# Two pad tiles that move the tile starts, gate weights decoded earlier in batch 0, and three subtractions one product later, in an attention and two-MLP kernel

## The chip, the core and the metric

One core of a Trainium2 chip runs the whole program. The metric is the time of the slowest core on the device in microseconds (us); with one core it is that core's time. All data is float32; f32r names the form in which TensorE takes float32 at the rate that this kernel uses.

## The reference

Eight batches of eight heads, 576 tokens, head size 64; 32 packed queries. Attention is done twice, first by the packed queries over the keys, then by the tokens over the packed result. Two MLPs over all 4608 tokens follow.

```python
def sm_attn(qq, kk, vv):
    s = scale * np.matmul(qq, kk.transpose(0, 1, 3, 2))
    s = s - np.max(s, axis=-1, keepdims=True)
    a = np.exp(s)
    a = a / (np.sum(a, axis=-1, keepdims=True) + 1e-09)
    return np.matmul(a, vv)
p_packed = sm_attn(p, k, v)
out = sm_attn(q, p_packed, p_packed)
x = np.ascontiguousarray(attn_out.transpose(0, 2, 1, 3)).reshape(B * S, H * D)
# first MLP, d_model 512, d_ff 1536
g = x @ w_gate
silu = g * (1.0 / (1.0 + np.exp(-g)))
val = x @ w_val
x = (silu * val @ w_out)
# second MLP, d_ff 2048
h = x @ w_in
g = h * np.cos(h)
out = g @ w_out
```

## The kernel before

TensorE multiplies in f32r by three passes: each operand is split into a high half (a copy on ScalarE that rounds to f32r) and a low half (a subtraction on VectorE), and high x high, high x low, low x high are added in PSUM (`PASSES`). The weights come from the host as int64 views and are decoded on the chip.

**Stage 1, attention and the first up projection (`a_up`, about 109 to 470 us for batches 1 to 7).** For each batch b the loop runs over twelve blocks f of d_ff. In each, `half` makes the gate product `pg` and the value product `pv` (L502 in batch 0, plain float32; L513 in the others, 12 f32r matmuls of 288 columns each), a silu on ScalarE (L533) and a product on VectorE (L553) give `h`, and a DMA from the POOL queue stores it. The weights of the up projection are first multiplied into the packed attention result (`a_wp`, `a_wp0_pair`, L473), so the products take the attention weights a2 as moving operand and `wp` as weights. The attention of batch b + 1 is done in the gaps: `sched` holds, for each half step k (k = 2f after pg, 2f + 1 after pv), the functions that are called there, and `attention` is handed a tuple of k for 18 steps: exponential, sum, transpose, packed product, its scaling, its transpose, second scores, turn, maximum, subtraction, exponential, sum, scaling, turn back, split, and three weight products. A split's low half is put into `pend` and issued at the next half step.

**Batch 0** (up to about 109 us) decodes the gate weights besides. There are 24 units, two for each block; `u_load` (SP queue, L315, four buffers of two units each), `u_act` (two ACTIVATEs on ScalarE, L108 and L109) and `u_dve` (two instructions on VectorE, L115 and L118) each have a counter, and `u_step(k, n)` moves one of the three on by n units. `a_wp0_pair(m)`, called in block f = 2m - 1 after the silu, multiplies the units 4m to 4m + 3 and copies the product to `wpp`, which the next two blocks use. PSUM has four tiles of two banks for all of this.

**Stage 2, the first down projection (470 to 740 us).** Strassen's scheme with seven products over five sets of tokens (`SETS`, four of 512 columns and one of 256), in the order `ORDER` = 0, 4, 6, 1, 2, 3, 5. `strassen` issues 36 f32r matmuls (L633); `sums1` issues on VectorE the subtractions of input blocks (L613) that product `i` of the set has in its table; `prep` makes the halves of the next product's input (L86 on ScalarE, L87 on VectorE), and `evict` follows. The input blocks `hr` are loaded from DRAM on the SP queue. The weights of product 0 lie in pool `da`, those of 3 and 5 in `db`, those of 4, 6, 1 and 2 in `gates` (`W1_AT`). The g tiles, the moving operand, lie in `da` and `db`.

**Stage 3, the second MLP (740 to 1497 us).** 48 steps p: seven products of six f32r matmuls with 384 columns (L959; weights `up` in pool `late`, moving operand `xs` in pool `xs`), a cosine on ScalarE and VectorE, and the down projection in pieces of twelve matmuls with 512 columns (L974; both operands in `late`). Inside a step, products and downs alternate.

**Where tiles start.** Pools are laid from the left (`cst`, `st`, then `att`, later `da`, `db`, `late`) and from the right (`gates`, `ups`, later `xs`). `cst` and `st` hold many small tiles before the left pools. Counted within a partition, all large tiles of the left pools start at 384 bytes past a multiple of 512, all large tiles of the right pools at 480 past one; a tile's inner pieces lie a multiple of 512 bytes from its start, but for a2 (multiples of 128).

Of the kernel before, what the change touches and what calls it, by code (L numbers as in the profile page):

```python
# [45 lines left out]
def attention_mlp_kernel(ctx: ExitStack, tc: tile.TileContext, qT, kT, vP, pP, wgv, w12, out):  # L46
# [7 lines left out]
    def pool(n, side=None):  # L54
        kw = {"side": side} if side else {}
        return stage[n].enter_context(tc.tile_pool(name=n, bufs=1, reuse_waits="tile", **kw))

    att = pool("att")
    gw, ups = pool("gates", "right"), pool("ups", "right")
# [277 lines left out]
    def u_step(k, n):  # L337
        for _ in range(n):
            (u_load, u_act, u_dve)[k](u_next[k])
            u_next[k] += 1  # L340
# [147 lines left out]
    def a_up(b, sched):  # L488
# [31 lines left out]
        for f in range(NF1):  # L520
# [32 lines left out]
            DVE.tensor_tensor(out=h_, in0=s_, in1=pv[:, :, :HS], op=ALU.mult)  # L553
            nc.gpsimd.dma_start(out=h1[f, :, S * b:S * b + S], in_=h_.rearrange("p c n -> p (c n)"))
            if b == 0:
                u_step(0, 1)
                u_step(1, 1)
                if f == 0:
                    u_step(2, 1)
                del wp[0, f]  # L560
            side(2 * f + 1)
# [40 lines left out]

    def sums1(s_, i):
        todo = {
            0: [((0, 1), (0, 1), (0, 0), fp) for fp in range(3)],
            2: [((1, 1), (1, 1), (0, 1), fp) for fp in range(3)],
            3: [((0, 0), (1, 1), (0, 0), fp) for fp in range(3)],
            4: [((1, 0), (1, 0), (1, 1), 0)],
            5: [((1, 0), (1, 0), (1, 1), fp) for fp in (1, 2)],
        }  # L610
        for to, x, y, fp in todo.get(i, ()):
            to, x, y = (raw1[s_, k, t, fp] for k, t in (to, x, y))
            DVE.tensor_tensor(out=to, in0=x, in1=y, op=ALU.subtract)  # L613
# [111 lines left out]
    with tc.manual_schedule():  # L725
# [46 lines left out]
            s2_mul(u)  # L772
            s2_back(0, u)
        s2_split(0)
        u_step(1, 2)
        u_step(2, 3)

        def loads(b, what):
# [11 lines left out]
        def first_scores(sched, b, at_k):  # L790
            put(sched, at_k[0], lambda: s1_mm(b))
            put(sched, at_k[1], lambda: s1_max(0), lambda: s1_max(1))
# [12 lines left out]
        for b in range(B):  # L805
            sched = {}
            if b == 0:
                for k, what in ((0, "k"), (6, "v"), (10, "q")):
                    put(sched, k, loads(1, what))
                first_scores(sched, 1, (4, 5))  # L810
                attention(sched, 1, (6, 8, 8, 10, 11, 12, 14, 15, 16, 17, 17, 18, 19, 20, 20, 16, 18, 21))
                first_scores(sched, 2, (22, 23))
                for k, what in ((17, "k"), (22, "v")):
                    put(sched, k, loads(2, what))
# [1 line left out]
            else:  # L816
# [4 lines left out]
                if b == 1:  # L821
                    put(sched, 2, loads(2, "q"))
                if b < B - 1:
                    attention(sched, b + 1, (0, 3, 3, 5, 6, 8, 10, 11, 12, 13, 14, 16, 17, 18, 19, 15, 17, 20))
                    for k, what in ((4, "k"), (8, "v"), (13, "q")):
                        put(sched, k, loads(b + 2, what))
                    if b < B - 2:
# [283 lines left out]
```

## Time and profile before

| | us |
|---|---|
| median of 3 runs | 1499.68 (1497.85 to 1500.71) |
| the profiled execution | 1502.94 |
| its span | 1501.1 |
| TensorE (PE) busy | 1468.8 |
| VectorE (DVE) busy | 1084.3 |
| ScalarE (ACT) busy | 850.0 |

The prediction's sum is made against the profiled execution. In the rows, PE is the matmuls, PEld the weight loads that overlap them, L12 a line of the kernel before. A matmul's own duration holds its run through the array, which overlaps the next one's; the time that it costs is the distance from its start to the next start. "PEclk" is the granted share of TensorE's full clock of 2.4 GHz; 0.50 is its lower level, 1.2 GHz. Idle time in square brackets stands with what ended it.

### The profile page before, as it was taken

To read this page: it belongs to the slowest core of one execution; us is meant where nothing else is said; L and a number is where in the kernel's file an instruction comes from. 1 tells how busy PE (TensorE), PEld (TensorE's weight loads), DVE (VectorE), ACT (ScalarE), POOL (GpSimd) and SP (SyncE) were. 2 spreads that over 40 slices of the span, in tenths; PEclk is the share of its full clock that TensorE was granted. 3 is DMA by queue.
4 is the path that set the end of the run, shared out by engine and by line. 5 is a ranking of instruction groups with operands and counts; after the bars stand their busy time and mean duration, and the time that the engine had idled before them with its cause. 6 is when DMAs were issued, how large, how long until landed. Compare 5 with 4: busy or idle time off the path is not lost.

```text
span 1501.1 us, 25026 instructions
## 1 busy us (share of the span) xinstructions
PE 1468.8 (98%) x9352; PEld 1262.1 (84%) x9352; DVE 1084.3 (72%) x1767; ACT 850.0 (57%) x1496; POOL 123.7 (8%) x230
## 2 busy tenths in 40 slices
PE   8999999999998999999999999999999999999998
PEld 6558878887887888898889989999999999999997
DVE  6567788788774788988776866776676686677654
ACT  5757666666653456554575646646465564664642
POOL 0002222222221011011000000000000000000000
PEclk9999999999999999999999999999999999999999
DMA  8938778877697558355495585576657558556641
GB/s 318 312 112 322 249 263 302 293 254 266 235 359 281 182 188 288 124 199 194 133 365 169 197 291 179 174 239 204 213 189 249 170 187 287 186 175 197 203 154 42
DMA packets 140937, 335.62 MB, mean 224 GB/s; under 512 B 15249, under 2 KB 25489, under 8 KB 140817
## 3 DMA queue, kind: packets, MB, share of 16 engines
q1 hardware_dynamic: 120720, 262.19, 52.7%
q0 software_dynamic: 20096, 71.84, 12.5%
q8 instruction: 74, 1.21, 0.3%
q14 instruction: 47, 0.38, 0.1%
HBM read 252.71 MB, written 81.26 MB: 222 GB/s over the span
## 4 chain that ended last, share of the span: by engine, by line
PE 81%; DVE 5%; ACT 4%; issue 2%; DMA 2%; SPq 0%; POOL 0%; DVEq 0%; ACTq 0%; POOLq 0%
PE acc L974 26%; PE p L959 23%; PE o L633 16%; PE pv L513 6%; PE pg L513 6%; PE wp L473 2%; DMA hr<-h 1%; DMA h<-h 1%; DVE wp L99 1%; DVE h L553 1%; PE pp L210 1%; ACT silu L533 0%; DVE d L287 0%; PE pv L502 0%; ACT wp L96 0%
## 5 line engine op out<-in xcount | busy, mean ns | idle before, releaser
L974 PE MATMUL acc<-wd,g 128*128 128x512 f32 x1728 | 418.1, 392 | 0.0
L959 PE MATMUL p<-xs,up 128*128 128x384 f32 x2016 | 379.1, 339 | 3.1 <-issue 1.6
L974 PEld LDWEIGHTS acc<-wd,g 128*128 128x128 f32 x1728 | 323.2, 188 | 61.3
L959 PEld LDWEIGHTS p<-xs,up 128*128 128x128 f32 x2016 | 359.1, 188 | 14.8 <-issue 1.9
L633 PE MATMUL o<-g,w 128*128 128x512 f32 (+1 forms) x1260 | 265.6, 373 | 4.3 <-DVE g L87 4.2
L633 PEld LDWEIGHTS o<-g,w 128*128 128x128 f32 x1260 | 220.6, 189 | 49.0 <-DVE g L87 5.5
L937 ACT ACTIVATE t<-c,quarter 128x384 f32<-128x384 f32 x144 | 88.5, 614 | 201.5 <-DVE c L1047 195.7
L513 PEld LDWEIGHTS pg<-a,wp 128*128 128x128 f32 x1008 | 137.4, 188 | 27.5 <-issue 10.9
L86 ACT ACTIVATE g<-hr 128x1024 fp32r<-128x1024 f32 (+1 forms) x105 | 101.9, 975 | 97.8 <-PE o L633 58.8
L513 PE MATMUL pg<-a,wp 128*128 128x288 f32 x1008 | 152.3, 300 | 3.2 <-DVE h L553 2.9
L513 PEld LDWEIGHTS pv<-a,wp 128*128 128x128 f32 x1008 | 137.7, 188 | 16.7 <-DVE w2c L398 3.0
L513 PE MATMUL pv<-a,wp 128*128 128x288 f32 x1008 | 150.6, 298 | 0.2
L87 DVE TENSOR_TENSOR g<-hr,g 128x1024 fp32r<-128x1024 f32 (+1 forms) x105 | 114.2, 1115 | 40.4 <-ACT g L86 40.2
L553 DVE TENSOR_TENSOR h<-silu,pv 128x576 f32<-128x576 f32 x96 | 71.5, 745 | 68.9 <-PE pv L513 21.9
L533 ACT ACTIVATE silu<-pg 128x576 f32<-128x576 f32 x96 | 62.5, 651 | 97.2 <-PE pg L513 84.7
L1042 DVE TENSOR_TENSOR u<-v,p 128x384 f32<-128x384 f32 x48 | 26.6, 554 | 120.8 <-PE p L959 120.1
L947 DVE TENSOR_TENSOR g<-t,g 128x384 fp32r<-128x384 f32 x192 | 106.1, 553 | 8.6 <-ACT g L934 8.5
L939 DVE TENSOR_TENSOR t<-t,k 128x384 f32<-128x384 f32 x192 | 106.2, 553 | 3.4 <-ACT k L943 1.8
L940 ACT ACTIVATE t<-t 128x384 f32<-128x384 f32 x192 | 98.2, 512 | 2.5 <-DVE t L939 2.4
L934 ACT ACTIVATE g<-t 128x384 fp32r<-128x384 f32 x192 | 98.6, 513 | 0.4 <-DVE t L945 0.4
L988 DVE TENSOR_TENSOR oacc<-oacc,acc 128x512 f32<-128x512 f32 x108 | 73.8, 684 | 34.6 <-PE acc L974 34.6
L943 ACT ACTIVATE k<-t 128x384 int32<-128x384 f32 x192 | 97.9, 510 | 0.0
(106 smaller groups left out, 1476.1 us busy)
## 6 DMA issues: line engine op xcount, KB each, us to landing
up<-w2u SPq DMA_DIRECT2D x336, 256.0 KB, 3.1
wd<-w2d SPq DMA_DIRECT2D x96, 512.0 KB, 6.1
h<-h POOLq DMA_DIRECT2D x96, 288.0 KB, 4.4
hr<-h SPq DMA_DIRECT2D x48, 512.0 KB, 6.9
raw<-in_w SPq DMA_DIRECT2D x44, 512.0 KB, 4.3
raw<-in_wgv SPq DMA_DIRECT2D x24, 512.0 KB, 6.4
w2u<-w2p POOLq DMA_DIRECT2D x24, 512.0 KB, 5.1
w<-w1u SPq DMA_DIRECT2D x21, 512.0 KB, 10.2
```

The costliest lines, as they stand in the source:

```text
L86: ACT.activation(out=hi, in_=src, func=AF.Copy)
L87: eng.tensor_tensor(out=lo, in0=src, in1=hi.bitcast(F32), op=ALU.subtract)
L513: PE.matmul(out=p_[:, c, :HS], lhsT=w[:, u, x, o:o + 128], rhs=a2[b][:, u, y, HS * c:HS * c + HS], start=(n == 0), stop=(n == 5),)
L633: PE.matmul(out=acc[:, m, :N], lhsT=wd1[n, fp][:, j, 256 * x + 128 * m:256 * x + 128 * m + 128], rhs=g1[n, fp][:, y, j, :], start=(first a ...
L934: ACT.activation(out=three["g"][:, 0, :], in_=three["t"], func=AF.Copy)
L937: ACT.activation(out=now["t"], in_=now["h"], func=AF.Identity, scale=1.0 / TWO_PI, bias=quarter)
L939: DVE.tensor_tensor(out=one_["t"], in0=one_["t"], in1=one_["k"], op=ALU.subtract)
L940: ACT.activation(out=one_["t"], in_=one_["t"], func=AF.Sin, scale=SIN_SCALE)
L943: ACT.activation(out=now["k"], in_=now["t"], func=AF.Copy)
L947: DVE.tensor_tensor(out=three["g"][:, 1, :], in0=three["t"], in1=three["g"][:, 0, :].bitcast(F32), op=ALU.subtract)
L959: PE.matmul(out=out, lhsT=w[:, u, 128 * k:128 * k + 128], rhs=x[:, v, k, :], start=(first and k == 0 and i == 0), stop=(last and k == 1 an ...
L974: PE.matmul(out=acc, lhsT=gs[p, a, t][:, x, o:o + 128], rhs=wd[j, f][:, y, :], start=(f == 0 and n == 0), stop=(f == 3 and n == 2),)
```

## The change

Two tiles that nothing reads are allocated: 120 floats at the right end, ahead of `gates`, and 32 floats in `cst`. With them all large tiles of both sides start at a multiple of 512 bytes, and a2's inner pieces at multiples of 128. Batch 0's `u_step` calls move units on earlier: one unit more on ScalarE ahead of the loop, and in the second half of f = 1, 2 and 3 one unit more for the load and for ScalarE and one for VectorE; the total of 24 is the same. Batch 1's loads and attention steps stand up to two half steps earlier. In batches 2 to 7 the split and the third weight product stand one half step earlier. The three subtractions that `sums1` made with product 0 of a set are made with product 1 in that order (number 4).

```diff
+    pad = ctx.enter_context(tc.tile_pool(name="pad", bufs=1, side="right"))
+    pad.tile([128, 120], F32, name="right_pad")
+    cst.tile([128, 32], F32, name="left_pad")
...
             if b == 0:
-                u_step(0, 1)
-                u_step(1, 1)
-                if f == 0:
+                u_step(0, 2 if f in (1, 2, 3) else 1)
+                u_step(1, 2 if f in (1, 2, 3) else 1)
+                if f in (0, 1, 2, 3):
                     u_step(2, 1)
...
         todo = {
-            0: [((0, 1), (0, 1), (0, 0), fp) for fp in range(3)],
+            1: [((0, 1), (0, 1), (0, 0), fp) for fp in range(3)],
...
         s2_split(0)
-        u_step(1, 2)
+        u_step(1, 3)
         u_step(2, 3)
...
-                first_scores(sched, 1, (4, 5))
+                first_scores(sched, 1, (3, 4))
...
-                    attention(sched, b + 1, (0, 3, 3, 5, 6, 8, 10, 11, 12, 13, 14, 16, 17, 18, 19, 15, 17, 20))
+                    attention(sched, b + 1, (0, 3, 3, 5, 6, 8, 10, 11, 12, 13, 14, 16, 17, 18, 18, 15, 17, 19))
```

What stands in a row on ScalarE in batch 0, from the silu of f = 2 on; `dec` and `wg` are a gate unit's two steps, E the exponentials of batch 1's first scores, wpp the copy of a pair's product. Before:

```order
L533 ACTIVATE silu_482<-pg_475 128x576
L108 ACTIVATE dec_486<-raw_454 128x512
L109 ACTIVATE wg_456<-raw_454,low3_87 128x2x256
L108 ACTIVATE dec_518<-raw_454 128x512
L109 ACTIVATE wg_471<-raw_454,low3_87 128x2x256
L533 ACTIVATE silu_536<-pg_529 128x576
L465 ACTIVATE wpp_443<-wp_538 128x1024
L108 ACTIVATE dec_551<-raw_484 128x512
L109 ACTIVATE wg_550<-raw_484,low3_87 128x2x256
L184 ACT_TABLE_LOAD
L184 ACTIVATE E_562,sm_564<-s1_489,nm_523 128x576
```

Here the silu of f = 3 (the second one) comes after two units. The same place of the changed kernel, whose lines stand four further down:

```order
L537 ACTIVATE silu_515<-pg_508 128x576
L112 ACTIVATE dec_519<-raw_480 128x512
L113 ACTIVATE wg_518<-raw_480,low3_92 128x2x256
L112 ACTIVATE dec_552<-raw_480 128x512
L113 ACTIVATE wg_551<-raw_480,low3_92 128x2x256
L112 ACTIVATE dec_555<-raw_548 128x512
L113 ACTIVATE wg_518<-raw_548,low3_92 128x2x256
L188 ACT_TABLE_LOAD
L188 ACTIVATE E_560,sm_562<-s1_490,nm_532 128x576
L188 ACTIVATE E_564,sm_566<-s1_491,nm_536 128x576
L537 ACT_TABLE_LOAD
L537 ACTIVATE silu_575<-pg_568 128x576
```

Three units, both exponentials and two table loads now stand ahead of the silu of f = 3; the exponentials stood after it.

On VectorE at the last gate units of batch 0, around f = 7 and 8; mx2 is the maximum of the second scores and d1 <- d1,mx2 its subtraction. Before:

```order
L266 TENSOR_REDUCE mx2_834<-d1_786 128x36
L115 SCALAR_TENSOR_TENSOR wg_782<-dec_831,wg_782 128x2x256
L118 SCALAR_TENSOR_TENSOR wg_782<-raw_780,wg_782 128x2x256
L553 TENSOR_TENSOR h_854<-silu_829,pv_847 128x576
L99 TENSOR_TENSOR wp_845<-wp_836,wp_845 128x2x512
L271 TENSOR_TENSOR d1_786<-d1_786,mx2_834 128x1152
L115 SCALAR_TENSOR_TENSOR wg_816<-dec_857,wg_816 128x2x256
L118 SCALAR_TENSOR_TENSOR wg_816<-raw_780,wg_816 128x2x256
```

After:

```order
L119 SCALAR_TENSOR_TENSOR wg_734<-dec_773,wg_734 128x2x256
L122 SCALAR_TENSOR_TENSOR wg_734<-raw_752,wg_734 128x2x256
L257 STREAM_TRANSPOSE d1_789<-s2_790 128x576
L257 STREAM_TRANSPOSE d1_789<-s2_791 128x576
L119 SCALAR_TENSOR_TENSOR wg_754<-dec_786,wg_754 128x2x256
L122 SCALAR_TENSOR_TENSOR wg_754<-raw_752,wg_754 128x2x256
L557 TENSOR_TENSOR h_836<-silu_815,pv_829 128x576
L270 TENSOR_REDUCE mx2_839<-d1_789 128x36
L275 TENSOR_TENSOR d1_789<-d1_789,mx2_839 128x1152
```

The last two units stood after the maximum and after the subtraction; now both stand ahead of the maximum.

On VectorE where stage 2 begins; h is the last product of stage 1, g the low halves that `prep` makes, hr the subtractions of `sums1`, p the additions of `evict`. Before:

```order
L553 TENSOR_TENSOR h<-silu,pv 128x576
L87 TENSOR_TENSOR g<-hr,g 128x1024
L613 TENSOR_TENSOR hr<-hr 128x1024 x3
L87 TENSOR_TENSOR g<-hr,g 128x1024 x6
L646 TENSOR_TENSOR p<-p,o_5766 128x512 x2
```

After:

```order
L557 TENSOR_TENSOR h<-silu,pv 128x576
L91 TENSOR_TENSOR g<-hr,g 128x1024 x4
L617 TENSOR_TENSOR hr<-hr 128x1024 x3
L91 TENSOR_TENSOR g<-hr,g 128x1024 x3
L650 TENSOR_TENSOR p<-p,o_5768 128x512 x2
```

The three subtractions stood ahead of the second product's three halves and now stand behind them.

## Rows read from the trace of the kernel before

**Rows 1.** Page, part 1: busy time, share of the span, instructions.

```profile
PE 1468.8 (98%) x9352; PEld 1262.1 (84%) x9352; DVE 1084.3 (72%) x1767; ACT 850.0 (57%) x1496; POOL 123.7 (8%) x230
```

**Rows 2.** Stretches: length, busy time by engine (count), PEclk, DMA share, GB/s. Stage 3.

```profile
740.30:1496.70 756.40, 753.34 (x3745) 680.35 (x3743) 515.69 (x982) 418.33 (x887) 1.08 (x2) 1.00 0.63 205
```

**Rows 3.** Page, part 5: groups by line, busy us, mean ns | idle before.

```profile
L974 PE MATMUL acc<-wd,g 128*128 128x512 f32 x1728 | 418.1, 392 | 0.0
L959 PE MATMUL p<-xs,up 128*128 128x384 f32 x2016 | 379.1, 339 | 3.1 <-issue 1.6
...
L633 PE MATMUL o<-g,w 128*128 128x512 f32 (+1 forms) x1260 | 265.6, 373 | 4.3 <-DVE g L87 4.2
...
L513 PE MATMUL pv<-a,wp 128*128 128x288 f32 x1008 | 150.6, 298 | 0.2
```

**Rows 4.** Stretches of L633 alone, PE: products 3,5,0; 6,1,2; 0; 6,1,2 (256 columns).

```profile
518.42:542.91 24.49, 24.49 (x110) 1.00 0.71 257
551.34:575.83 24.49, 24.49 (x106) 1.00 0.45 159
651.42:655.73 4.31, 4.31 (x37) 1.00 0.44 172
660.15:672.97 12.82, 12.82 (x110) 1.00 0.46 154
```

**Rows 5.** Timeline of PE in stage 3: start, length, instructions.

```profile
1215.48 3.35 PE L959 MATMUL p<-xs,up 128*128 128x384 f32 x18
1218.67 2.91 PE L974 MATMUL acc<-wd,g 128*128 128x512 f32 x12
1221.41 2.28 PE L959 MATMUL p<-xs,up 128*128 128x384 f32 x12
1223.53 2.92 PE L974 MATMUL acc<-wd,g 128*128 128x512 f32 x12
1226.29 2.28 PE L959 MATMUL p<-xs,up 128*128 128x384 f32 x12
```

**Rows 6.** Timeline of PE in stage 1.

```profile
363.20 1.76 PE L513 MATMUL pv<-a,wp 128*128 128x288 f32 x12
364.80 1.75 PE L513 MATMUL pg<-a,wp 128*128 128x288 f32 x12
```

**Rows 7.** Waits of PE from 20 to 109 us: total, times, longest.

```profile
PE wp L473 <- DVE wg L118: 7.1, 7, 2.9
```

**Rows 8.** Timeline of PE in batch 0; in brackets the idle time before.

```profile
35.54 1.06 PE L473 MATMUL wp<-wg,ppT 64*32 64x512 f32 x8 [0.99 <-DVE wg L118]
36.78 1.06 PE L473 MATMUL wp<-wg,ppT 64*32 64x512 f32 x8 [0.18 <-DVE wg L118]
...
92.11 3.63 PE L473 MATMUL wp<-wg,ppT 64*32 64x512 f32 x24 [2.92 <-DVE wg L118]
```

**Rows 9.** Stretches in batch 0; the last three numbers are PEclk, DMA share, GB/s.

```profile
64.00:68.00 4.00, 4.00 (x91) 2.56 (x84) 0.37 (x1) 2.63 (x4) 0.00 (x0) 0.60 0.83 251
...
92.00:96.00 4.00, 3.89 (x25) 0.93 (x26) 1.88 (x4) 3.03 (x4) 0.00 (x0) 0.50 0.02 4
96.00:100.00 4.00, 4.00 (x13) 2.98 (x13) 0.93 (x2) 0.90 (x1) 0.00 (x0) 0.76 0.00 0
```

**Rows 10.** Groups by line, shapes apart: a gate unit's steps on ScalarE, a table load.

```profile
L109 ACT ACTIVATE wg<-raw,low 128x512 int32<-128x512 uint8 x24 | 18.3, 761 | 0.0
...
L108 ACT ACTIVATE dec<-raw 128x512 f32<-128x512 f32 x24 | 16.0, 669 | 2.2 <-DMA raw<-in_wgv 2.2
...
L184 ACT ACT_TABLE_LOAD x7 | 9.0, 1283 | 0.4 <-DVE nm L176 0.3
```

**Rows 11.** Timeline at the head of stage 2, VectorE and PE.

```profile
482.02 4.62 DVE L87 TENSOR_TENSOR g<-hr,g 128x1024 fp32r<-128x1024 f32 x4
...
483.30 28.97 PE L633 MATMUL o<-g,w 128*128 128x512 f32 x116 [4.16 <-DVE g L87]
```

**Rows 12.** Stretch of set 0's second product; L633 alone, PE and PEld.

```profile
478.74:493.12 14.38, 10.22 (x37) 7.84 (x36) 0.88 1.06 394
```

More of the change, by code (lines that the diff above doesn't have):

```diff
@@ L807, in attention_mlp_kernel @@
             if b == 0:
-                for k, what in ((0, "k"), (6, "v"), (10, "q")):
+                for k, what in ((0, "k"), (4, "v"), (8, "q")):
                     put(sched, k, loads(1, what))
-                first_scores(sched, 1, (4, 5))
-                attention(sched, 1, (6, 8, 8, 10, 11, 12, 14, 15, 16, 17, 17, 18, 19, 20, 20, 16, 18, 21))
+                first_scores(sched, 1, (3, 4))
+                attention(sched, 1, (5, 7, 7, 9, 10, 11, 13, 14, 15, 16, 16, 18, 19, 20, 21, 16, 18, 20))
                 first_scores(sched, 2, (22, 23))
```

## Prediction

> **What bounds the kernel now.** I read the busy times first: TensorE holds 98% of the span [rows 1], and in the last stage it holds 753.34 of 756.40 us [rows 2]. So only two things can shorten the program: a shorter matmul, or a stretch in which TensorE waits or runs at a lower clock. Then I read the groups by line for the counts: 1728 and 2016 matmuls in the last stage, 1260 in stage 2, 2 x 1008 in stage 1 [rows 3]. All these are f32r; 7020 of them.
>
> Next I looked at how long one such matmul takes from start to start, for each place of its operands in the memory. The tile starts are in the section on the kernel: left pools start at 384 past a multiple of 512 bytes, right pools at 480. Stage 2 is the test, since one line there draws its weights from both. In 24.49 us, 110 matmuls were seen with weights at 384 (products 3, 5, 0) and 106 with weights at 480 (6, 1, 2); the moving operand starts at 384 in both. Two were in flight at the edge, so 108 and 104: 226.8 against 235.5 ns [rows 4]. The same with 256 columns: 4.31 us for 36 is 119.7 ns, 12.82 us for 108 is 118.7 ns [rows 4]. The order of work and the shapes are equal; the place is what differs. The 384-384 pairs lie on a line: (226.8 - 119.7) / 256 = 0.418 ns a column, and 226.8 - 512 x 0.418 = 12.8 ns fixed, say 13.
>
> In stage 3 the moving operand xs starts at 480 and the weights at 384: 18 + 12 matmuls of 384 columns take 3.19 + 2.12 us, 177.0 ns each; the downs take 2.74 and 2.76 us for 12, 229.2 each, though their operands both start at 384 [rows 5]. By the line they would take 160.5 + 13 = 173.5 and 226.8. In stage 1 both operands start at 480 or 128 bytes steps from it, and 12 matmuls take 1.60 us, 133.3 ns [rows 6]; the line gives 120.4 + 13 = 133.4. So an f32r matmul costs its columns plus 13 ns where weights and moving data sit alike against 128 bytes, and something else where they don't.
>
> Then the waits. In batch 0 TensorE waits 7.1 us in seven pieces for decoded gate weights [rows 7]; the first two, 0.99 and 0.18, and the last and longest, 2.92, are shown [rows 8]. Around them the granted clock falls from 2.4 towards 1.2 GHz: 0.60 in 64 to 68 us, 0.50 in 92 to 96, 0.76 in 96 to 100 [rows 9]. At the head of stage 2 it waits 4.16 us for the low half of the second product's input, which VectorE could write only at 482.02, after sums whose data had landed late [rows 11]; that product takes 14.38 us at a mean clock of 0.88 [rows 12].
>
> **Part 1, the pads.** Two tiles that nothing reads; no instruction. Afterwards all large tiles start at 0 against 512 bytes, so weights and moving data sit alike everywhere. No row shows f32r at 0, so this is bounded from the rows. The value I take is that 0 behaves as 384 does with 384, since that is the nearest row in kind (weights and moving data alike, the same line and shape):
> - L959: (173.5 - 177.0) x 2016 = -7.1 us.
> - L974: (226.8 - 229.2) x 1728 = -4.1 us. These start alike already; I put their excess down to the stream of products that they alternate with, a guess.
> - L633, products 4, 6, 1, 2 (576 matmuls of 512 columns): (226.8 - 235.5) x 576 = -5.0 us; 144 of 256 columns: +0.1.
> - L513: 133.3 to 133.4, nothing.
>
> Sum -16 us. From below: the fixed 13 ns goes as well (a rival). From above: 0 is a bad place (a rival), or no place matters (a rival). For VectorE, ScalarE and DMA I take nothing: no wait that ends late hangs on their speed by so little. The trace bears on a rule here. The Trainium skill, "SBUF — State Buffer", section "Who interferes with whom", gives TensorE two read ports of its own, one for weights and one for moving data, and says that "PE and ACT never wait on anyone"; its 16-byte lines divide 384 and 480 alike. By that the pads would change nothing. The 8.7 ns of [rows 4] speak against it.
>
> **Part 2, decoding ahead in batch 0.** One unit more before the loop, and one more on each queue in the second half of f = 1, 2, 3; in all still 24 units. By the order, the unit that pair 5 needs stood behind the softmax subtraction on VectorE and now stands before the maximum; for pairs 2 to 5 all units are queued a half step or more before TensorE asks. Pair 1's waits stay (VectorE's queue up to there is the same): 7.1 - 0.99 - 0.18 = -5.9 us. The low clock follows these gaps: 0.40 x 4 + 0.50 x 4 + 0.24 x 4 = -4.6 us [rows 9].
>
> What is late next: on ScalarE three units of 0.669 + 0.761 us, two exponentials and two table loads of 1.283 us [rows 10] now stand between the silu of f = 2 and that of f = 3. The three units and the loads alone are 6.9 us, where TensorE has some 7 us of work (two half products of f = 2 and one of f = 3 at 2 us, the pair at 1). Two of the four PSUM tiles hold the first scores until the exponentials are done, so the second half of f = 3 and then the input of f = 4 (a copy behind that silu) wait; the copies of the transposed weights wait behind f = 3's three units. I put these new waits at 2 us, bounds 0 and 6. The loads go earlier too: SP issues the gate units 9 to 23 and the v and q tiles of batch 1 up to two steps sooner, and behind a load that waits for its buffer stand those tiles. DMA engines were busy 0.83 in 64 to 68 us and 0.02 in 92 to 96 [rows 9], so they end early enough to be pulled forward by some 10 us. Batch 0: -5.9 - 4.6 + 2 = -8.5 us, bounds -12 and -4.
>
> **Part 3, sums a product later.** The four low halves now stand before the three sums. The first needs nothing that comes late (its copy on ScalarE stands ahead of the waits), so TensorE should go on at 478.74, where the first product ends. A product with weights alike is 36 x 226.8 ns = 8.2 us, so 14.38 - 8.2 = -6.2 us [rows 4, 12], the low clock within it. The sums' next reader is the second set of sums, after product 6's input: the data came by 482, three sums and three halves at 1.2 us each (4.62 us for four, [rows 11]) end near 487, when product 4 ends. In sets 1 to 4 the sums move from one product to the next, which then holds some 11 us of VectorE work against 8.2; three tiles of input stand ready, so I take 0, bound +1 a set.
>
> **Part 4, batches 2 to 7.** Split and third weight product half a step earlier in six batches. Each moved product brings its copy on ScalarE and its low half of 1.2 us on VectorE ahead of an h product, whose bank a matmul then waits for. Either way under 0.7 us a batch: I take 0, bounds -3 and +4.
>
> **Sum.** -16 - 8.5 - 6.2 = -31 us. The profiled execution took 1502.94 us (span 1501.1); 1472. The median of the runs stands 3.26 us lower: 1469.
>
> **Rivals.**
> - *The place doesn't matter at 0.* What I read as place is a pattern of pools. For it: one line, two pools. Against: the same split shows in every set. Parts 2 and 3 alone: 1499.7 - 14.7 = 1485. Chance 0.17.
> - *The 13 ns goes too.* A start 128 bytes off the 512 would then cost it. Against: it is the same at 384 with 256 and 512 columns, as a fixed cost of a new weight would be. The excess over columns is now 16.5 x 2016 + 15.2 x 1728 + 21.5 x 576 + 13 x (432 + 252 + 2016) = 107 us; all gone, 1499.7 - 107 - 15 = 1378. Chance 0.08. The Trainium skill, "TensorE: Matmul & The Clock Gate", section "Back-to-back issue gap", has a warm gap of N / 2.4 + 2.5 ns; by that 7020 x 2.5 = 18 us of it would stay, an estimate: 1396. No row here shows f32r so near its columns.
> - *Slower: alike at 0 is a collision.* Weights and moving data then start in the same 512 bytes, and each f32r matmul pays what the 480 weights pay now, 21.5 ns over its columns: L959 +5.0 x 2016 = 10, L974 +6.3 x 1728 = 11, L633 +8.7 x 432 = 4, L513 +8.6 x 2016 = 17; 42 - 15 = +27, 1527. It decides from 15 us / 7020 = 2.1 ns a matmul. Against: alike at 384 is the good case. Chance 0.08.
> - *The decoding moves a wait instead of ending it.* ScalarE's block before the silu of f = 3 holds TensorE for 6 us or more, the clock falls again, and batch 0 gains about nothing: 1477. Chance 0.12.
>
> **How the numbers follow.** The forecast, 1469, has 0.55; its own range, by the bounds of the parts, is 1456 to 1482. The first and the last rival lie close above it, so 1455 to 1489 leaves out the two rivals of part 1 at either end and a little more, 0.2. A measurement of this kernel tells 0.2%, 3 us, from no change. Faster by that: 0.55 + 0.17 + 0.08 + 0.12 less a little, 0.90; within: 0.02; slower: 0.08.
>
> **What would show it.** Right: in stage 2 both windows hold the same number of matmuls, 24.5 us for 108; products of 18 in 3.12 us and downs of 12 in 2.72; no wait for a gate weight after 37 us and a clock of 1.00 from 60 to 100 us, stage 1 beginning some 8 to 10 us sooner; the second product of stage 2 in 8.2 us. Wrong: counts that stay at 110 and 106 (no effect of place), 1.60 us for 12 in stage 1 falling well under that (the 13 ns moves), or a gap before f = 4 of batch 0 longer than the one before pair 5 was.

## The result, and the profile after

The changed kernel takes 1478.63 us in the median (1477.73 to 1480.73), the kernel before 1499.37 beside it: a ratio of 0.9864, 95% interval 0.9847 to 0.9881. That is 20.7 us less, where 31 had been forecast. The interval is some 2.5 us wide to either side, and those of the runs below are much the same; what is said of smaller differences rests on the traces. The profiled execution took 1480.73 us, its span is 1478.6.

The stages, by the first matmul of each in the two traces, the tail from the start of the last one (us):

| | before | after | difference | forecast |
|---|---|---|---|---|
| batch 0 | 108.90 | 96.16 | -12.7 | -8.5 |
| stage 1 | 361.64 | 361.54 | -0.1 | 0 |
| stage 2 | 269.73 | 261.53 | -8.2 | -11 |
| stage 3 | 756.39 | 754.91 | -1.5 | -11 |
| tail | 4.49 | 4.46 | 0 | 0 |

The differences add up to -22.5 and not to -20.7, since the profiled execution of the kernel before lay further above the median of its runs (3.3 us) than that of the changed kernel (2.1). And the -8.2 of stage 2 hold a loss that belongs to the entry of stage 3: by the starts, the last product of stage 2 takes 10.94 us until the first product of stage 3, where it took 8.16. Without these 2.78 us stage 2 gained 11.0, as forecast.

Busy time and the three costliest groups of f32r matmuls, from the page after (parts 1 and 5; its lines stand four further down than before's in [rows 1, 3]):

```profile
PE 1456.0 (98%) x9352; PEld 1257.3 (85%) x9352; DVE 1082.6 (73%) x1767; ACT 849.8 (57%) x1496; POOL 123.7 (8%) x230
...
L978 PE MATMUL acc<-wd,g 128*128 128x512 f32 x1728 | 419.1, 392 | 0.0
L963 PE MATMUL p<-xs,up 128*128 128x384 f32 x2016 | 378.3, 338 | 3.9 <-issue 2.6
...
L637 PE MATMUL o<-g,w 128*128 128x512 f32 (+1 forms) x1260 | 258.9, 368 | 0.0
```

The 4.3 us wait of the first down projection [rows 3, 11] is gone. The group of the downs (the pieces of the second MLP's down projection) became 1.0 us longer, not shorter, and the products of stage 3 have a wait of 2.6 us.

Stage 2, the two stretches that answer to the first two of [rows 4]: matmuls of L637 alone (length, busy and count, PEclk, DMA share, GB/s), products 3, 5, 0 and then 6, 1, 2.

```profile
498.51:522.99 24.48, 24.48 (x110) 1.00 0.71 257
531.15:555.63 24.48, 24.48 (x110) 1.00 0.43 157
```

Equal counts, as the prediction wanted. From start to start, a matmul of 512 columns in stage 2 now takes 226.7 ns in all seven products. Products 4, 6, 1 and 2 had taken 8.43 us for 36, or 234.2 ns, not the 235.5 that the prediction read from the counts in its window. And set 0's second product, which took 14.38 us [rows 12], takes 8.16 at full clock:

```profile
465.87:474.03 8.16, 8.16 (x38) 6.76 (x37) 1.00 1.05 407
```

Stage 3, PE's timeline at the place in a step that answers to [rows 5]: 12 products, 12 downs.

```profile
1199.64 2.27 PE L963 MATMUL p<-xs,up 128*128 128x384 f32 x12
1201.75 2.92 PE L978 MATMUL acc<-wd,g 128*128 128x512 f32 x12
1204.51 2.27 PE L963 MATMUL p<-xs,up 128*128 128x384 f32 x12
1206.62 2.92 PE L978 MATMUL acc<-wd,g 128*128 128x512 f32 x12
```

12 products take 2.11 us, 175.8 ns each (177 before), and 12 downs 2.76, 230 each (229.2 before); 173.5 and 226.8 had been forecast. Cut by place in the step, the starts of the trace show why. A product that follows a product takes 173.3 ns a matmul, each of its six. A product that follows a down takes 171, 175, 177, 185, 176, 182: 177.6 in the mean. The twelve of a down that follows a product take 229, 233, 236, 224, 231, 236, 228, 233, 231 and then 227, 227, 227. The pattern repeats to a nanosecond through the stage. So the line of 13 ns plus columns holds in a settled stream, and after each change of width six products or nine downs are off it.

Batch 0, two stretches of the trace before and two of after (the columns are length, busy time of PE, PEld, DVE, ACT and POOL with counts, PEclk, DMA share, GB/s). Before:

```profile
0.00:60.00 60.00, 52.59 (x456) 37.00 (x457) 36.19 (x71) 37.05 (x59) 3.40 (x14) 1.00 0.91 323
60.00:108.90 48.90, 43.90 (x350) 25.70 (x349) 31.49 (x42) 27.38 (x38) 3.79 (x7) 0.90 0.49 167
```

After:

```profile
0.00:60.00 60.00, 52.91 (x533) 37.31 (x534) 41.43 (x79) 42.40 (x68) 3.41 (x14) 1.00 0.93 342
60.00:96.16 36.16, 36.16 (x274) 22.46 (x272) 26.20 (x34) 21.98 (x29) 3.79 (x7) 1.00 0.49 195
```

From 60 us on TensorE no longer waits, and its clock no longer falls. The waits of PE in batch 0 from 20 us on (total, times, longest) show what came in place of the 7.1 us of [rows 7]:

```profile
PE pv L506 <- ACT E L188: 1.6, 1, 1.6
...
PE wp L477 <- DVE wg L122: 0.8, 2, 0.7
```

One wait for the exponentials of the first scores, which hold PSUM while ScalarE decodes, is new; it is the wait that the prediction took at 2 us.

How much low clock the waits bring differs from one execution to the next. Five traces hold batch 0 as it was (the kernel before and four of the runs below), each with the same 7.1 us of waits: batch 0 takes 108.9, 105.7, 106.3, 109.1 and 105.4 us in them, with 10.2, 3.4, 3.4, 10.2 and 0 us at 1.2 GHz. Six traces hold the new order: 96.2, 96.3, 97.4, 97.7, 96.1 and 98.3 us. Their means lie 10.1 us apart, so some 2.6 of the 12.7 are owed to the two traces that the table compares.

What the prediction had not looked at is the entry of stage 3. PE's timeline, after:

```profile
707.83 8.78 PE L637 MATMUL o<-g,w 128*128 128x512 f32 x38
719.23 11.06 PE L963 MATMUL p<-xs,up 128*128 128x384 f32 x46 [2.62 <-issue]
```

and before:

```profile
740.27 1.21 PE L959 MATMUL p<-xs,up 128*128 128x384 f32 x6
743.05 3.24 PE L959 MATMUL p<-xs,up 128*128 128x384 f32 x17 [1.57 <-issue]
```

Before, the first product started at once and the second waited 1.57 us; now the first waits 2.62. The waits end 0.1 us behind the last additions of stage 2, which read the last accumulator. VectorE's timeline has them, after and then before:

```profile
717.85 1.27 DVE L650 TENSOR_TENSOR p<-p,o 128x512 f32<-128x512 f32 x2
...
741.68 1.28 DVE L646 TENSOR_TENSOR p<-p,o 128x512 f32<-128x512 f32 x2
```

By the order in which the kernel's PSUM tiles come free, that accumulator lies in the first pair of banks in the changed kernel, and the first product of stage 3 is given the first bank; before, it lay in the last pair, which the second product was given. The trace doesn't show banks; a run below tests this. In the profiled execution the granted clock was at 1.2 GHz behind this gap, from 718.6 to 725.4 us:

```profile
718.60:725.40 6.80, 6.17 (x19) 6.20 (x20) 1.12 (x3) 0.49 (x1) 1.08 (x2) 0.50 0.94 309
```

A matmul of 384 columns takes 320 ns from start to start in this stretch instead of 175, and the start of the stretch falls into the wait; added up, the low clock cost 2.9 us. The mean clocks of the other three executions, 1.000, 1.000 and 0.999, leave room for none or part of that.

### The profile page after: what moved, and what is told of

Read it like the earlier page. It is cut to its first block, busy times and chain, and to the rows that moved or that the text cites. A ratio compares the mean times of both kernels' runs of the same rounds, so it can differ in the third digit from the quotient of the medians.

```text
span 1478.6 us, 25027 instructions
## 1 busy us (share of the span) xinstructions
PE 1456.0 (98%) x9352; PEld 1257.3 (85%) x9352; DVE 1082.6 (73%) x1767; ACT 849.8 (57%) x1496; POOL 123.7 (8%) x230
## 4 chain that ended last, share of the span: by engine, by line
PE 85%; DVE 6%; ACT 5%; issue 3%; DMA 1%; POOL 0%; SPq 0%; ACTq 0%; DVEq 0%; POOLq 0%
PE acc L978 27%; PE p L963 23%; PE o L637 17%; PE pv L517 6%; PE pg L517 5%; PE wp L477 2%; PE pv L506 1%; PE pg L506 1%; DVE wp L103 1%; PE pp L214 1%; DVE d L291 1%; DMA h<-h 1%; ACT wp L100 1%; PE s L247 1%; DVE af L298 1%
## 5 line engine op out<-in xcount | busy, mean ns | idle before, releaser
L637 PE MATMUL o<-g,w 128*128 128x512 f32 (+1 forms) x1260 | 258.9, 368 | 0.0
L637 PEld LDWEIGHTS o<-g,w 128*128 128x128 f32 x1260 | 219.4, 189 | 39.2
L951 DVE TENSOR_TENSOR g<-t,g 128x384 fp32r<-128x384 f32 x192 | 105.7, 551 | 8.6 <-ACT g L938 8.4
L944 ACT ACTIVATE t<-t 128x384 f32<-128x384 f32 x192 | 98.3, 512 | 2.5 <-DVE t L943 2.4
```

The costliest lines, as they stand in the source:

```text
L637: PE.matmul(out=acc[:, m, :N], lhsT=wd1[n, fp][:, j, 256 * x + 128 * m:256 * x + 128 * m + 128], rhs=g1[n, fp][:, y, j, :], start=(first a ...
L944: ACT.activation(out=one_["t"], in_=one_["t"], func=AF.Sin, scale=SIN_SCALE)
L951: DVE.tensor_tensor(out=three["g"][:, 1, :], in0=three["t"], in1=three["g"][:, 0, :].bitcast(F32), op=ALU.subtract)
```

## The experiments

### The parts alone

**The pads alone** (`pads_only`): the kernel before with

```diff
+    pad = ctx.enter_context(tc.tile_pool(name="pad", bufs=1, side="right"))
+    pad.tile([128, 120], F32, name="right_pad")
+    cst.tile([128, 32], F32, name="left_pad")
```

> The kernel before with the two pad tiles alone; nothing else is changed. By the prediction's first part, -16 us against the kernel before: 7.1 on the seven products of stage 3, 4.1 on its downs, 5.0 in stage 2. By the theory formed from the two traces (a start in the same place brings a matmul down to its columns plus 13 ns only in a settled stream, and the first nine or so matmuls after a change between 384 and 512 columns stay off that line wherever their operands start): about -6 us, with stage 2 at 226.7 ns a matmul of 512 columns in all seven products, the first product after a down still near 177.6 ns a matmul, the one behind it at 173.3, and the downs near 230. If the gain seen came from the schedule alone and the place does nothing, 0.

Measured: 1494.07 us against 1500.20, ratio 0.9962 (0.9947 to 0.9977): -6.1. By start-to-start means of the trace L633 gives (226.8 - 231.1) x 1008 + (120.1 - 119.4) x 252 = -4.2, the products of stage 3 (175.2 - 176.7) x 2016 = -3.0, the downs (230.1 - 229.5) x 1728 = +1.1. The sum is -6.1; that it meets the measured time to 0.1 is luck, since that is known to some 2 us. The theory of the settled stream holds; the -16 do not.

**Batch 0 alone** (`batch0_only`): the kernel before with the `u_step` calls and the tables for batch 1 as in the change.

```diff
-                u_step(0, 1)
+                u_step(0, 2 if f in (1, 2, 3) else 1)
...
-                attention(sched, 1, (6, 8, 8, 10, 11, 12, 14, 15, 16, 17, 17, 18, 19, 20, 20, 16, 18, 21))
+                attention(sched, 1, (5, 7, 7, 9, 10, 11, 13, 14, 15, 16, 16, 18, 19, 20, 21, 16, 18, 20))
...
```

> The kernel before with batch 0's calls that move gate units on and batch 1's attention steps as in the changed kernel; no pads, no change to the sums. By the prediction's second part -8.5 us, bounds -12 to -4. By the trace of the changed kernel batch 0 ends 12.7 us sooner, and the entry of stage 3 is about 1 us later than before (its first product writes the PSUM bank that the last accumulator of stage 2 holds, which this schedule alone brings about), with up to 3.4 us more where the clock falls behind that gap: -12 to -8 us. By the rival that decoding only moves the wait: 0.

Measured: 1492.40 against 1500.20, ratio 0.9956 (0.9942 to 0.9970): -7.8. Batch 0 ends at 96.34 us in its trace, as in the changed kernel, so decoding ahead needs no pads. And the entry of stage 3 is the bad one here too:

```profile
725.68 1.98 PE L633 MATMUL o<-g,w 128*128 128x512 f32 x8
730.28 6.00 PE L959 MATMUL p<-xs,up 128*128 128x384 f32 x24 [2.62 <-issue]
```

With the pads alone and with the sums alone the first product starts at once, so it is this part of the change that brings the wait. How it does so is argued from the kernel: the other order of steps in batch 1 makes PSUM tiles come free in another order, the four tiles rotate differently from there on, and the rotation is still off 600 us later.

**The sums alone** (`sums_only`):

```diff
-            0: [((0, 1), (0, 1), (0, 0), fp) for fp in range(3)],
+            1: [((0, 1), (0, 1), (0, 0), fp) for fp in range(3)],
```

> The kernel before with the first subtractions of each set one product later; no pads, batch 0 as before. By the prediction's third part -6.2 us: the second product of stage 2 takes 8.2 us instead of 14.38 where the weights lay alike; here they still start at 480, so 36 x 235.5 ns = 8.5 us, -5.9, with no low clock at its place. If the wait goes on to the second set of sums or to product 6, it comes back there and the gain is 0 to -3.

Measured: 1493.29 against 1500.78, ratio 0.9946 (0.9932 to 0.9960): -7.5. The first three products run through:

```profile
468.00 25.20 PE L633 MATMUL o<-g,w 128*128 128x512 f32 x108
```

The second takes 8.43 us (476.18 to 484.61), 5.95 less than the 14.38; stage 2 takes 262.75 us instead of 269.73. Nothing is late next: in sets 2 to 4 the second product, too, is 0.2 to 0.4 us shorter, which makes most of the last 1.0 us.

The three runs add up to -21.4 us, and the whole change gave -20.7. The edit of batches 2 to 7 was not run alone. That it is worth little rests on stage 1's length: 361.64 us before, 362.05 with batch 0's part alone, 361.54 with the whole change.

### What "alike" means

**Both sides at 384** (`pads_384`): the right pad has 24 floats, no left pad.

```diff
+    pad.tile([128, 24], F32, name="right_pad")
```

> The kernel before with one pad of 24 floats at the right end: the tiles of the right pools move from 480 to 384 past a multiple of 512 bytes, the left ones stay at 384; nothing else is changed. If it counts that weights and moving operand start alike, the same gain as with both sides at 0, -5 to -8 us, and stage 2 at 226.7 ns in all seven products. If the multiple of 512 itself counts, the products whose both operands moved only from 480 to 384 gain nothing beyond what the kernel before has where both start at 384; that is the same 226.7 in stage 2, but 12 matmuls of stage 1 and the 384 columns of stage 3 would stay above what both sides at 0 give.

Measured: 1494.44 against 1500.20, ratio 0.9963 (0.9950 to 0.9976), the same as with both at 0. Stage 2 (226.8), products (175.3) and downs (230.1) agree with the pads' run to 0.1 ns. The multiple of 512 is nothing special.

**The right side at 0, the left at 384** (`pads_mixed`): the right pad of 120 floats alone.

```diff
+    pad.tile([128, 120], F32, name="right_pad")
```

> The kernel before with the right pad of 120 floats alone: right pools at 0, left pools at 384 past a multiple of 512 bytes, so weights and moving operand start alike against 128 bytes and differ against 512; nothing else is changed. If 128 bytes count: -5 to -8 us as with both at 0. If 512 bytes count: within 2 us of the kernel before, with products 4, 6, 1 and 2 of stage 2 still near 235 ns a matmul.

Measured: 1494.20 against 1500.20, ratio 0.9960 (0.9945 to 0.9975). The total, -6.0, is what "128 bytes count" had expected, and its reason is another. In stage 2 the same work takes unequal time (L635 is this kernel's L633; first products 6, 1, 2, then 3, 5, 0):

```profile
489.17:514.36 25.19, 25.19 (x110) 1.00 0.39 132
514.36:538.84 24.48, 24.48 (x109) 1.00 0.70 257
```

108 matmuls take 25.19 us with the starts 128 bytes apart, 233.2 ns each, against 226.7. So 128 bytes are not enough. But stage 3 is shorter than in any kernel so far, 751.31 us:

```profile
734.99:1486.30 751.31, 748.18 (x3745) 677.69 (x3743) 515.16 (x982) 418.30 (x887) 1.08 (x2) 1.00 0.63 207
```

Its downs, whose own operands had not moved, went from 229.5 to 227.9 ns a matmul; what had moved are the products ahead of them. The second of the two small kernels below tests whether that is the cause.

**Streams by place** (`probe_place`): a small kernel of its own.

```python
def stream(name, w, m, N, count):
    for i in range(count):
        if i % 12 == 0:
            acc = ps.tile([128, 512], F32, tag="b", name=name)
        wo = w // 4 + 128 * (i % 6)
        mo = m // 4 + 512 * (i % 12)
        PE.matmul(out=acc[:, :N], lhsT=W[:, wo:wo + 128], rhs=X[:, mo:mo + N],
                  start=i % 12 == 0, stop=i % 12 == 11)
```

> No part of the reference is computed; it writes zeros and runs streams of 48 f32r matmuls of one width back to back, each with its own starts of weights and moving operand against a multiple of 512 bytes (s512_w384m0 is 512 columns, weights at 384, moving operand at 0), with 12 matmuls at 0 and 0 between them. If only the difference of the two starts counts, and against 512 bytes: columns times 0.418 plus 13 ns (226.7, 173.3 and 133.3 ns for 512, 384 and 288) wherever both start alike, at 384 or 480 or 64 as at 0, and 2 to 9 ns more at most of the other pairs; a difference of 128 with 384 columns near 175.5, as the run with the right pad alone shows it. If the difference against 128 bytes counts: (384, 0), (128, 0), (256, 0) and (0, 384) at 226.7 too. If the multiple of 512 itself counts: only (0, 0) on the line. If the 13 ns belong to the place: some pair falls below 220 for 512 columns.

PE's timeline of its first streams of 512 columns (the names lose their last number: these are weights, moving operand at 0, 0; 384, 384; 480, 384):

```profile
23.15 11.04 PE L47 MATMUL s_w0m<-X,W 128*128 128x512 f32 x48
34.03 2.89 PE L47 MATMUL base<-X,W 128*128 128x512 f32 x12
36.76 11.05 PE L47 MATMUL s_w384m<-X,W 128*128 128x512 f32 x48
47.65 2.89 PE L47 MATMUL base<-X,W 128*128 128x512 f32 x12
50.38 11.39 PE L47 MATMUL s_w480m<-X,W 128*128 128x512 f32 x48
...
61.60 2.91 PE L47 MATMUL base<-X,W 128*128 128x512 f32 x12
```

From a stream's start to the start behind it: 10.88, 10.89 and 11.22 us for 48, or 226.7, 226.9 and 233.8 ns. All pairs, worked out in this way (a few matmuls behind each change of place are in the means):

| moving start minus weight start, modulo 256 bytes (pairs weights/moving) | 512 columns, ns | 384 columns, ns |
|---|---|---|
| 0 (0/0, 384/384, 256/0, 480/480, 64/64) | 226.7 to 227.5 | 173.3 to 173.9 |
| 32 (0/32) | 233.4 | 173.3 |
| 64 (0/64) | 229.2 | 173.2 |
| 96 (0/96, 384/480) | 233.6, 233.4 | 176.6, 176.5 |
| 128 (0/384, 384/0, 128/0) | 232.4 to 233.2 | 175.9, 176.0 |
| 160 (96/0, 480/384) | 234.2, 233.9 | 173.5, 173.4 |
| 192 (64/0, 96/32) | 233.3, 233.4 | 176.6, 174.7 |
| 224 (32/0) | 233.2 | 173.4 |
| 240 (16/0) | 226.7 | 173.5 |

The first three expectations each fail in part. It is the difference of the starts, but modulo 256: 256/0 lies on the line, the one pair that tells 256 from 512 there. One pair, 96/32, doesn't fit into that at 384 columns. No pair falls under 226.7, so at 512 columns the 13 ns do not belong to the place. With 288 columns every pair lies between 131.5 and 133.4 ns. The line would give 133.3; the pairs with a difference of 0 take 131.6 to 131.7, so the line doesn't hold for this width.

**Two widths in turn** (`probe_switch`): the same small kernel, with groups of two widths.

> No part of the reference is computed; it writes zeros and runs groups of f32r matmuls of two widths in turn, with starts as the name tells (p384x18m128_512x12: 18 of 384 columns with the moving operand at 128, 12 of 512 at 0), without any other engine at work. If the change of width itself sets the excess of stage 3: one width alone stays on the line (173.3, 226.7); 18 of 384 and 12 of 512 in turn give about 230 ns over the twelve and 174.7 over the eighteen, as in stage 3; groups of 42 and 36 show the same excess in nanoseconds at each change, and one of each in turn is worst. If the rest of the kernel (transfers, VectorE, ScalarE) causes it: both widths on the line in every case. If the starts of the products set what the downs behind them pay, as the run with the right pad alone suggests (227.9 for downs whose own operands had not moved): the case with the moving operand at 128 gives near 228 where both at 0 gives 230.

PE's timeline; a case holds 108 matmuls of 384 columns and 72 of 512, and d has both operands of both widths at 0, n has the starts of the kernel before, p and s the moving operand of the 384 columns at 128 and at 64:

```profile
97.43 35.60 PE L65 MATMUL d384x_512x<-X,W 128*128 128x384 f32 x180
132.87 5.60 PE L65 MATMUL base<-X,W 128*128 128x512 f32 x24
...
319.02 33.36 PE L65 MATMUL l512s_512s<-X,W 128*128 128x512 f32 x144
352.22 5.65 PE L65 MATMUL base<-X,W 128*128 128x512 f32 x24
...
398.61 35.72 PE L65 MATMUL n384x18m_512x12s<-X,W 128*128 128x384 f32 x180
434.16 5.61 PE L65 MATMUL base<-X,W 128*128 128x512 f32 x24
...
480.45 35.52 PE L65 MATMUL p384x18m_512x<-X,W 128*128 128x384 f32 x180
515.81 5.60 PE L65 MATMUL base<-X,W 128*128 128x512 f32 x24
...
602.93 35.28 PE L65 MATMUL s384x18m_512x<-X,W 128*128 128x384 f32 x180
638.05 5.60 PE L65 MATMUL base<-X,W 128*128 128x512 f32 x24
```

By the line, 108 x 173.3 + 72 x 226.7 ns is 35.04 us. Measured: d 35.44, n 35.55, p 35.36, s 35.12. In d the two widths take 174.7 and 230.1 ns, in n 176.8 and 228.7, in p 175.5 and 227.9, in s 173.4 and 227.7. These are stage 3's own numbers, with no transfer and no other engine at work (DMA share 0.00 from 40 us on), so neither causes them. And in p only the products' moving operand lies elsewhere than in d, and the downs go from 230.1 to 227.9, as with the right pad alone. One width alone stays on the line (173.7 over 72 of 384 columns, 226.7 over 72 of 512), and groups of 42 and 36 come down to 173.9 and 227.8, so the excess of d belongs to the change of width: (35.44 - 35.04) / 6 = 67 ns for each change there and back. It is not the only change that costs. In l all 144 matmuls have 512 columns, in groups of twelve with both operands at 0 and both at 96 in turn; they take 33.20 us instead of 32.64, 93 ns there and back. And not every change of width does: 384 and 256 columns in turn take 21.10 us where the lines give 21.12. One of each in turn, expected to be worst, gave 174.8 and 231.7, little more than d. And an operand start that is best for the one width alone is not the best for the two in turn: 64 costs the 384 columns nothing and takes away most of what the downs pay.

### The entry of stage 3, and a better kernel

**The entry mended** (`entry_both`): the changed kernel with

```diff
+                if end and i == 4:
+                    keep_busy(1)
                 evict = strassen(s_, i)
...
                     for n in range(7):
+                        if n == 4:
+                            evict()
                         split_x2(n, x_now)
-                evict()
+                if not (end and i == 6):
+                    evict()
```

> The changed kernel with a short dummy matmul ahead of the fifth product of the last set of stage 2, which moves the last accumulator from the first to the last pair of PSUM banks, and with the last product's additions ahead of the last three splits of stage 3's input instead of behind them. If the 10.94 us of the last product are the wait for its own PSUM bank to be read: stage 3 starts within 0.5 us of that product's end, the wait at its second product is under 0.8 us, the clock stays at 1.00 through 718 to 726 us, and the whole takes 1475 to 1477 us against 1478.6. If something else holds stage 3's first product (its input, its weights), the gap of 2.6 us stays and the time with it.

Measured: 1476.24 us, ratio 0.9837 (0.9821 to 0.9854), 2.4 less than the changed kernel, though the two intervals overlap. PE around the entry, and VectorE's last additions:

```profile
718.35 1.22 PE L968 MATMUL p<-xs,up 128*128 128x384 f32 x6
718.55 1.28 DVE L650 TENSOR_TENSOR p<-p,o 128x512 f32<-128x512 f32 x2 [1.32 <-PE o L637]
...
719.94 4.23 PE L968 MATMUL p<-xs,up 128*128 128x384 f32 x23 [0.36 <-issue]
```

The last product of stage 2 takes 8.16 us instead of 10.94, the wait behind the first product is 0.36, and stage 3 takes 752.95 us instead of 754.91, with no low clock. It was the read of the accumulator's bank that stage 3 waited for. The run holds both mends at once, so what each is worth alone isn't shown; in the timeline the additions now start as soon as the last product ends, and the first product no longer waits for them.

**The input of the second MLP at 128** (`xs_128`): the changed kernel with

```diff
+                    DVE.memset(late["x"].tile([128, 96], F32, tag="shift", name="shift", bufs=1), 0.0)
```

> The changed kernel with the tiles of the second MLP's input at 128 past a multiple of 512 bytes instead of 0 (a tile of 384 bytes in its pool, and one short write to it); the weights of its products and all operands of the downs stay at 0. If only the difference of the starts counts, stage 3 takes what it took with the right pad alone, 751.3 us against 754.9, with downs near 228 and products near 175.5, and the whole about 1475.5 us. If both at one multiple of 512 is best, as the first part of the prediction had it: products at 177 again and the whole near 1482.

Measured: 1475.38, ratio 0.9834 (0.9819 to 0.9849). Stage 3:

```profile
720.70:1469.95 749.25, 747.99 (x3744) 677.83 (x3744) 512.50 (x978) 418.31 (x887) 0.79 (x2) 1.00 0.62 207
```

Products at 175.5 and downs at 227.9, as with the right pad alone. The difference of the starts carries over, from one pair of places to another. This kernel's entry is still the bad one, with a wait of 2.67 us, but the granted clock is 1.00 behind it, from 720.7 to 727.5 us.

**Both mends, and the input at 64** (`best`): `entry_both` with the tile above at 112 floats instead of 96.

> The changed kernel with both mends of stage 3's entry, as run before (a dummy matmul ahead of the last set's fifth product, the last additions ahead of three splits), and with the second MLP's input tiles at 64 past a multiple of 512 bytes. If the streams of the probe carry over (18 products of 384 columns with the moving operand at 64: 173.4 ns, the twelve downs behind them 227.7), stage 3 gains 1.85 x 2016 + 2.4 x 1728 = 7.9 us on the 752.95 that it takes with the entry mended, 745.1, and the whole takes 1476.2 - 7.9 = 1468.3 us. If the rest of the kernel disturbs the streams, it stays between 1468 and 1476.

Measured: 1469.03 us (1468.93 to 1470.58) against 1500.78, ratio 0.9790 (0.9777 to 0.9803). Stage 3 takes 745.81 us, 0.7 more than worked out; products 173.4 and downs 227.7 ns, as in the probe:

```profile
716.64:1462.45 745.81, 743.92 (x3745) 673.52 (x3743) 515.98 (x983) 417.61 (x887) 1.09 (x2) 1.00 0.62 208
```

This kernel is faster than the kernel before and than the changed one; its interval lies clear of both.

**Three downs in a row** (`best_three`): `best` with

```diff
-            step_down(p)
...
             swap_x(6)
-            step_down(p)
+            for _ in range(3):
+                step_down(p)
```

(the `step_down` calls behind products 2 and 4 are gone).

> As the kernel before it in this call, with the three downs of each step of stage 3 one behind another at the step's end, so that the width of the matmuls changes 2 times a step instead of 6. By the probe a change back and forth with the moving operand at 64 costs about 12 ns over twelve downs, so two fewer of them a step give 96 x 12 ns = 1.2 us, if no new wait appears; three accumulators and four products then share eight PSUM banks, and a wait of 0.1 us a step already costs 5 us. -1 to +10 us against the kernel before it in this call.

Measured: 1472.24 (1470.69 to 1475.61), ratio 0.9811 (0.9796 to 0.9825), 3.2 more than `best`. The downs do come down to 227.0 ns, 0.7 x 1728 = 1.2 us, as worked out. But at the first steps products wait, 3.0 us in all where `best` has 1.5, and in the profiled execution, the slowest of the four, the clock falls from 751.8 us for 3.4 us:

```profile
749.94 1.31 PE L969 MATMUL p<-xs,up 128*128 128x384 f32 x6 [1.34 <-ACT p L1044]
751.48 3.91 PE L969 MATMUL p<-xs,up 128*128 128x384 f32 x12 [0.23 <-DVE u L1051]
```

## Why the prediction was right in its sign and too large

- **Pads, stage 2 (-5.0):** right; -4.2 in the pads' own run. The term was a little large because 8.7 ns a matmul had been read where the starts give 7.5.
- **"Alike against 128 bytes":** this reading failed. With the starts 128 bytes apart a matmul of 512 columns takes 233.2 ns. The pads made all starts equal, so no term hung on it.
- **Pads, products of stage 3 (-7.1):** this term failed. It held a settled stream's 173.5 for all seven products. Four of seven are settled and take 173.3; three come behind a down and take 177.6: (4 x 173.3 + 3 x 177.6) / 7 = 175.1. The gain was -3.0.
- **Pads, downs (-4.1):** this term failed in its sign, +1.1. The prediction put the downs' excess down to the stream they alternate with, and called that a guess. The guess was right, and it spoke against the term: a change of width costs at equal starts too (67 ns in the probe), so pads that make all starts equal could not take it away.
- **Pads, stage 1 (0):** right; 132.7 to 132.8. That the line gave 133.4 there says little: in the probe it doesn't hold for 288 columns.
- **"0 behaves as 384 does":** right, shown by the run with both at 384.
- **Batch 0 (-8.5):** -12.7 in its stage. Idle time fell by 5.3 us (12.4 to 7.1) where 3.9 had been taken: the waits for gate weights went from 7.1 to 0.8, and the new wait measured 1.6 instead of 2. The low clock was worth about 0.10 x 48.9 = 4.9, where 4.6 had been taken; that the two agree is luck of this trace, since the same waits brought between 0 and 10.2 us of low clock in five traces. The remaining 2.5 us are TensorE's busy time. The trace with the right pad alone, whose batch 0 is the old one without any low clock, has 2.9 us more of it than the trace after: its weight products (`a_wp0_pair`) are busy 13.7 us instead of 9.5, at 600 and 599 ns a matmul. Matmuls of equal length that overlap less are what waits between them leave; this is argued.
- **Not in the sum: the entry of stage 3.** Batch 0's schedule costs there 1.05 us of wait, and 2.9 of clock in the profiled execution. The prediction followed who waits for PSUM within batch 0, not what another order of releases does to the rotation of the four tiles.
- **Sums (-6.2):** right; 5.95 on the second product.
- **Batches 2 to 7 (0):** stage 1 agrees.

So 11 us had been forecast for stage 3 and less than 2 came, which is most of what the total is short of. The entry of stage 3 took some more; batch 0, by the means of the traces 1.6 us above its term, gave part of it back, and that is luck.

The rivals: "the place doesn't matter at 0" fell with the 226.7 of products 6, 1 and 2. "The 13 ns goes too" fell with the probe, in which no place brings 512 columns under 226.7. The collision fell with the equal 226.7 at 0 and at 384. The decoding did make a wait, of 1.6 us, with no low clock in the trace of the changed kernel. In two of the other traces with this batch 0 (`xs_128` and `best_three`) 3.4 us at 1.2 GHz follow this wait, of 1.6 and 3.0 us there; they are far from taking the gain away.

Of the rule of the Trainium skill ("SBUF — State Buffer", section "Who interferes with whom"), by which TensorE never waits on anyone, the runs leave this: stage 3's excess appears with every other engine idle, so it is no wait on another engine; but the two operands' starts alone move a matmul of 512 columns by up to 7.5 ns.

## What to carry to other kernels

Measure what a matmul costs from start to start in the stream in which it runs, and cut it by its place in the pattern, before a cost per matmul is multiplied by a count; a mean over mixed streams hid here that the downs, once settled, were already on the line. Tile starts are worth trying for f32r streams, by the difference of weights and moving operand and for the real sequence of widths; a probe of a few streams forecast a gain of 7.9 us in stage 3, and 7.1 came. After a change of order, look at which PSUM bank meets which at the next stage's entry, however far away.

## What the runs showed of the hardware

- An f32r matmul with a new weight each time costs 226.7, 173.3 and 120.0 ns for 512, 384 and 256 columns at best: columns times 0.417 plus 13.3 ns, at every place that lies well. With 288 columns it is 131.6, 1.7 under that line. At 1.2 GHz a matmul of 384 columns took 320 ns, its columns times 0.833 and nothing more (stage 3's entry in the changed kernel).
- With 512 columns, starts that differ modulo 256 bytes by 32 or more, either way, cost 2.5 to 7.5 ns a matmul; weights that start 16 bytes past the moving operand cost nothing. With 384 columns, a moving operand 32, 64, 160, 224 or 240 bytes past the weights, modulo 256, costs nothing, and one 96, 128 or 192 bytes past them 1.4 to 3.3.
- After a change between 384 and 512 columns six or nine matmuls are off the settled time by -3 to +12 ns, in a pattern fixed to the nanosecond; how much in all depends on the starts of both widths (67 ns there and back with all at 0, 13 with one moving operand at 64). A change of both starts at one width cost as much (93 ns there and back), a change between 384 and 256 columns nothing. What inside TensorE or its reads makes it was not found.
- Waits of 2.62, 2.62 and 2.67 us at stage 3's entry were followed by 6.8 us at 1.2 GHz, by 3.4 us and by none, in the traces of the changed kernel, of batch 0 alone and of `xs_128`; 0.36 us was not followed by any fall.
